# One kernel, two written-out orders of the same 4,431 steps

## The chip, the cores and the metric

The kernel runs on one core of one Trainium2 chip. The metric is device time in microseconds (us) of one execution; a kernel's time is the median of several runs. The engines are PE (TensorE, matmuls), DVE (VectorE), ACT (ScalarE), POOL (GpSimd) and SP (SyncE, which here only starts DMAs). Each engine works through its own list in the order in which the program was written.

## The reference

Inputs are queries, keys and values of 8 batches x 8 heads x 512 positions x 64 (`q_l`, `k_l`, `v_l`), 32 global positions per head (`q_g`, `k_g`, `v_g`), and two weight matrices.

```python
s_g = scale * q_g @ concat(k_g, k_l).T          # global queries see all keys
out_g = softmax(s_g) @ concat(v_g, v_l)
s_ll = where(abs(i - j) <= 32, scale * q_l @ k_l.T, -1e9)
out_l = softmax(concat(scale * q_l @ k_g.T, s_ll)) @ concat(v_g, v_l)
x = concat(out_g, out_l)                        # to 4352 x 512: heads side by side
out = gelu_erf(x @ w_in) @ w_out                # 512 -> 2048 -> 512
```

All of it is fp32.

## The kernel before

**The work.** Attention is cut into 64 units (batch, half of the 512 positions, pair of heads), the MLP into 17 chunks of 256 rows: one for each (batch, half) and the last, "g", for the global rows. Nearly every fp32 product is done as three products of fp32r halves: a copy rounds a value (high part), a subtraction leaves the rest (low part). So each product brings a copy (ACT or DVE) and a subtraction (POOL or DVE) with it.

**Steps.** `graph()` names 4,431 steps. The ones that the text below speaks of:

- Of a unit: `lk`, `lq`, `lv` load keys, queries, values; `lh` loads the global queries of a batch (lines 741, 865); `tk`, `tq` transpose (on PE for the first eight units, L819 to L827); `k1`, `q1` copy and `k2`, `q2` subtract (L605 on ACT, L607 on DVE, L612 the subtraction); `s` is the score product (L906), `m` masks it and finds the maximum from PSUM (L925), `b` scales that (L931), `e` is exp on ACT (L779), `n` sums up and normalizes (L955, L956, L959), `nf`, `ns` fill edge tiles (L966, L971), `t` transposes (L980 to L983), `ah`, `al` split the result out of PSUM (L605, L1000), `vm`, `vc`, `vl` ready the values, `o` is the product with the values (L1017, L1030), `c`, `x` put it together (L1043, L1048, L1049).
- Of the weights: `wl` loads one of 32 pieces of 512 KB (L630, L634), `w1` to `w3` pack it (L639 to L651), `w4` copies the high part, `w5` subtracts (L612, tile `wl`).
- Of the MLP: `h` (in parts `hc`) and `mo` are the two products of the first five chunks (L1206 to L1212, L1352 to L1362), `g` is gelu on ACT (L779), `gh` copies its high part (L605 or L607), `gl` subtracts (L612). From the sixth chunk on two chunks at a time share sums and differences of the weights, made once: `sw`, `ss`, `sh`, `sl` compute these, `sx`, `ya` write them to DRAM (tile `wd`), `rl` fetches 512 KB of them (L1275, `rt<-wd`, 168 times), `ft`, `fh`, `fl` make the matching sums of x, and `P` is the product (L1314).

**Order.** `SEQ` is a packed list. `plan()` unpacks one number for each step: number divided by 6 is the step's place in `graph()`, the remainder is the engine. The main loop emits the steps in this order and ties each instruction to the one emitted before it on its engine, so an engine's list is the list of `SEQ` filtered by engine. `DUR`, `LAT` and the due times in `graph()` play no part when the kernel runs; the data dependences, the counts of buffers and the lists do.

**The port wait.** `PORT` names the kinds of step which on DVE read or write SBUF alone. After such a DVE step the next POOL step in `SEQ` gets a semaphore wait on it:

```python
if x["on"] == "p" and not x["size"]:
    if shared:
        tc.add_manual_dep(ins[seen], shared, ... reason="port")
    shared = None
elif x["on"] == "v" and x["port"]:
    shared = ins[-1].name
```

There is no wait in the other direction: a DVE step that comes after a POOL step in the list is not held by a semaphore until that is done.

**Buffers.** PSUM has six tiles that turn among scores, transposes and hidden sums (`u`), five SBUF tiles turn among `g`, `gh`, `gl` (`gg`). `FORMS` names, of 33 numbered weight slots, the ten whose tile is taken from the pool `wq` and not from `wp`; these slots are used again for other data later.

Of the kernel before, what the change touches and what calls it, by code (L numbers as in the profile page):

```python
# [138 lines left out]
JOINT = {"s": "u", "t": "u", "h": "u", "gh": "gg", "gl": "gg", "gf": "gg"}
FORMS = (3, 5, 7, 9, 17, 19, 21, 23, 25, 27)  # L140
# [8 lines left out]
    "KF>Z(fc-l`l@hY(gt;Xd?axEb*|{5v?&bGO-z*bX=ca3Cfjr@`aEe*nkf8h8>Z^Uyte;3kj8a|QVm{5(8>NFcI^ZseopKHz#_6k+pts=!r1&qeq(co`9>8mRgU*^9h^R8-xD&qBIA`+?`H{GLgOYQz^+_uy|"
    "<eO<K(c^eq<M5`VlS0d&h7a)5PFvN63A0qDgchxcEuT@Ck8pJ!uSCMZaUqoy`EJvz<0F(l~5jnex45E0csQ&_yUc6U}UR&h=ja9)=H>&0%GM*HWjXDT4qlY{tPY{hk2~bIN9#}?4(K+--$SJ5Fk<SB{AO;X_"  # L150
    "kRG@dNkmOV(=lbxd%#*R9*9NIKx))s#5B}q&vwra<WkTsBo$}{@-cq_r=a&DIhZY=(;z8o2*Cz@i~xW~JRbsQpiQV2&=-gb(2kmoK7gFyQDP+EX4Ep!NyL1#6*G#EV0IuD1K&hH1g=5%fcAJ!Bfkf32Z6yG("
    "0!<_z*9gV=ojQd^f+RQ2M#_9I*;(7Lf{Z;zh@TskSC711kz)Udv0T{Ae<N?@;>GfhUXQ4JeW;r81_2ibI?<uP81P)22DX0P(W-5^9lMD^e^Z?5pRHEm^N?(v<mzHu^nBFL?L&Br-Ob)C%|mvbWaaT4qgKuK>"
    "vXr!}fVb&_}RqQL90FKw2;ja2WkH7=yhI!hz}7c^((wTkzND<5)9z3LuBsjv2%Ok!eg0+>Kf2c^CXFcnrP7^Bh>|6?<0zmU&iqPN2ES5x{ECdQZ%I88Gg-jb>r>-bLV<m}fAPF>_GourHuCfv;o5$Rpr7Kmg"
    "F`9mk&YAgTmdZPgsiYp8Xo1sEB21xkZ0cn#R;fXmoM>?H3K^kvWIm^Faw9tdVJW(lgt>&7OkK0w{}JXbZ}dmp_N^KR85?|sikTo^mk`xa&ZbEHazT#B9Qy;JoiW*>$HbOI*>b;$QH7Gw){5VHqx8|y?q_Kac"
    "t$W6Fcfy0<#)Kc$U@9zM7)qwX128sC;cM`MG`y=Wz;5L+{Dvo^}o3A2ZGT0tp7j^{o3+5bZ6bJU+#lBSal&=q8!EV7}aAz<T+=o>st9IcYR$08$uq2$@`v&$gb_~~tU4RGUUd6BVZt$+b{>L{NyUDu>e+J0J"
    "&BH@#ws;TW=3@Ck1a2X=1t`SL^}#?pyo1<jz<>J|<Co*FVU`0oVx^!LeP01T!g{@RxD&WI=rnE+|FUnF7gaL}r@-lOeV{9-h!<A_@m<EDd={JycM(YNxp4v9=h(M>3EY_)4CraxI^XX&X3Yhhs74E-`l7h)*"
    "bjVJ&`jKV(0<UU_ZH|i-v<01>~0jf=1rds{~RcX8^(`$xiuevp5XSO?%=lK6*X6CcHxhB@6-T@eK->MZ`@(fJRHk+!VAIwhWZnQ!t;F+pB+plyofu5x(_1Ync#2mANjoCF7QG8E8wqu3<4Ry&&R{>#J`SH`C"
    "Rz<gcB$xeko2<bJ}~sE5T0!Z}Tbf5yJQQlX!E@6|bYlhd1Ca)`am<{0;A6-%8vUz8f`*NN4aJggf3O{z1(aFogI&@B^>E=9mxLLT>p1d=U@u8GLzsTg^2*hmfrC)G%7Cz6xI0@}uuA>IK3LywfKnocG<qzd}"
    "&9Oe77~_<RrX|Dd3ROFnH27>ywQ=F1R(gg<>SG#1Sz_L4%r&%oRk41qut6RE`Mqyph*Fd3~PvWV~1{D+jS86zwu@xfg+5<<*pYneuvN3yg`tmz|cCF+UGNIir}_|>G|8h6VSLfYqViL|H)@s@&*g%$yfgaX+"
    "@oQnUT#zt@v%%FR|Ov?~yX3YxHdXk?|YUwBR)qF<O`vEOZBG3OhVP4H<l8^WX;XA^MHLD4)*I4}%TJ{jc{!eO_)=X*XBZi49YqpXG3EOL?w~UY`lGT2fze1i%{DCl1^FHD0n!`1HEqh2Z%2>?|@_e$_4{GTp"  # L160
    "pQu?tj1rT?gQU%bNyI%Zv&oCdsFtZj17!zce~X54sO1#lc*}lL$nT`2{FjMf>RG}P@>x=z_%iVlDMZQpFB7g2I{X7<E5%DWMw-{Ml3XG3$=68>TPFFJ631Hxi0jF35!aGq6b$t?={+Ki`T_YC;S2I0ah&uw="
    "~MDm;*ypvWC8VD%WmR*!ZZG1;v>?smL9*DJW2$TPZCMwQSyKNQ2>HEMm|D4K)l?dAQP!f@);tWyrN}wOOkSwc#DW57bv|HK+Q}Fn|g=HCS7mQlfNhb$6uj5B+95J@;LPbb$!cF%jTBtEwB17QElYgEh8-(X{"
    "&*AC=2`t{3rcq{kN$=(oz5YmIvf2%5m~J>NvTX{ENShoFqT+|Kb0Qsvw;w|4x3{A0!J%_o>4)Kwt~)u3tsHLw?79%|DrPg}mGkAw5rdiSoDw><3ePR6NB*wNc&FA{7#N+mE220{s+f)qaYaR7=@Kd(YoM`pE"
    "wsg-Yq9E~oG*Vd^T%1S-N$2&|=iNco<!ffA?U{6A90XlT+D>SvTk)UA~Dbg~~zI~zdIh_v05=~N==H01*2D&;SVh+!qoqRyeNrtYA<OC6=%q%i%|04wkw{Wa<e>I>8(G#pLCSVDb7*+^xQrh*j=en3tW(p;o"
    "%)M2WhbU83WJx-fU)6s4PLZsgV0H&E{V|?P51itj2rgf0MqF$$gf^z~Rem{djyFla895hv6LBLHjG5)0aX>P_9S~dM%;7Q;anjx^C8ewEe@Zba5R62q=gSI%3r9GjMnTtUC{iI+U4Z@5uX43lu|D|!6V}QvF"
    "6x|w_#z@lU(Fk-LGs7s;@Ie}VA?+0!lfFFQ47^Db)0xaU^b$kF<kDvY254((eGD0M0z(*_PhS;q(sfKd-51zeWu>>!=Q33Em+1eaudba}Yi6#mbu*d47Z^ZbnWP9VtnH@<>5FSCRlHy*kfM(=t^)@HAJJFQ9"
    "n4p2m)CBgFJUZWY^>cF_?D4iW|;wIEbtj!A8ZH~=w)U)Pzb!qum@+bKB<k;ch^<|QRdI|F{U@Tit!!eea3G3aP1&t8{@Oui}V+Rn;9dF9~gUU=dmUSrUqsOh67`@*XgrauLlFcZu&&#h1#uwC9G476|6t#S8"
    "LY<KM1}TJOOgDv%#aaI|FAJ&oEyNPG>G;MS!PjZ`MwxpQ&BR^s)Pxml&_H+JdhzcL%OB-U`0M{3Q4s^RL>~tVPTqdwcLOGZh?U4KRmTqx6yBW>%8j72Fe~bJjB_1#dC-2Zxx4g4<bT_62a1eLVQEHpjltxC;"
    "IQyf<)+b%HsO&F35p>|~7xj|Tn%AE1BC{ElU2UFO(XK-S;jFPKN^AGW^L3S$AP$LVg?JvxSUD)4lWz=Bl=SSrpqYX@_biLd^o^<0p{!Bo?#*(@vP0iDVkY<<7=a`5xkSwR7-iXml5I3d>c;5pV;EDeiO-O1X"
    "|l2pf7s%jYH5z|opZ1BrgYqg;Ib`Z<%VKr5^R8L`}80OX*Mu`=vUJ!i3OjR2=j@DmU-?z?Sds?rtoSZ4F+3cH~n=Crx9*e>*R_|?{T78`}t9n;myxPMVX9ip6RzGH)XI^2>XD?)jI8&;BXD+B-!#=|XvF``z"  # L170
    "?8m`}oEYb&>hD^?t<hF!?K{<J4y+EreumRueV4PbdS~@3>^Ip}bthYe?A_IOm|RA(7127t-dFugE3S1#wSv95dVBT3>a(riSLZlat4HfLu&=fvYW1~*PIv7lHm2^cRt|fA-KpxE)wxzJ`&b<a@(KGF_JnFP`"
    "&`|jx^9lQw%j_I^J5(x!tW%vUaouCx}D8zz13>y{F;q{5Fx*^xvg&A>S|C()JlUWS|_$TJ8iuC)#s{3kP$Y%Rt*_r|H0-!sI}HwT`M$Xf)MJ$wai*c9lfr%bw=y#*4u19qz!VI&8wBvexByk(L$H2)pZ_-pz"
    "iCmk9UGSlfw=vAotmENEWg$U4-o95<4*=LFXI}qw_zICu~w^0cR^G#*5Y-PHSq({KwTujxh8&X98q?D}f{LOx1qDjdjk06lx2+*CB607IPZwOq~wMqSkWl($+PQLg%|_SKYc$h_@6n&^oC$#gm309Dm(6+@+"
    "kUo$k)5wG|$RZw#60hC=HhfzJ7Ly3qTOc<0BEk3){o04Gv+t!`iFP^i>-yY9uhA3|S2-s8N*0dl4MIi2_G{?)m-6VC00B<l7<206o=>7BbcIPOo7QO<86CjUHS2IK%|7X-*V0y)WfT(^jOlryh0UH1yNQ1>f"
    "j2gDijg?j21LC$a{@|M&MrTc1+rAgeg>E9t+>lxhF>jt<}>TW?+a6jNqtGgZgI}{3yr{T~O5EK97^cwEH^yPG4T`aV!GaXu9_csIp{Vk1$3iyT47OsZBfjgCl4bS5JnV!$v+PR<0<*uuHy>nIFr|Fk?b9h5_"
    "HvaN@5jV+Ia{uJ^^B_<bbZ;jW`cYk;yQK3l_epwt-CMlXoe#JtxbJpqxF)Wh3+i<8H+BAxM-FfA^l<(BU7g6zRrN<Z*Vdou3~<x@L0*Kvzq2-cyz^$~&iW6+zjneh@7BlpMShf9;#TuE)zdTQI-llF;EwaQg"
    "*Nh@<=*bBgm%@B)z9DxG9U3K@K4ll;f-_u?%ctf#s_2&ne*H)d7p>obI<V)@HCmx`m;PVZ!eFKIm%;Z4%h#}vt*v)pRRXjCWrd?Ux&`si!z79y3CKEE8Hc5EA=<(f8%*FINtsGdHg%|%LO-hcX*fhctLCCN&"
    "QFshrCP%%72l6lRG8Tmsuv58oJJpWd;Sg3{vn%W?^Pn0OX$wRWiSZW`!uc-VBQe5n%X>`G1B9^(!*3W;SPLXSh77V3pt|KPh~JzbNxhh*ZCt-_O6tKOYwJK;d=#Px*H<kNFz~TLnY>JsD8_%FH{NIU$x{V`e"
    "9RL8v6$$4As3;;VRDGQ0W5_z^*EJzuahQyqCqIL<$m=@5tnqnVtrPpA+~5b6a@0&&EXMTR-`R>2oxO5{kUE-VZ$4($+37pg=io==b#%o7#`22nD*K=?2ttT&64;oXA%&|X1Va71uW@Nsxz7L@%(utc~_I8m@"
    "Xv?}Bgtq@)nJQ4-!74@HmR|%scUv@M+Bb%<jDbR-R3LGMP_!)sed{S^C{9i#NyiOPp)eAooE)bj%{38Ge4}^z=vjj;|JPZ+L!Vs}F><j-KmJ7EDfnu7l6h1B<5r(s9;e>Fso+HfGUkN`5ch?ide}q}$JHkD}"  # L180
    "jEE@wTev8zsoyUwi%?>fuqt8@HVRvW6!ExtN;o2%C`xCiiyG?P!d_7^i;D2YXT*<%)uLBK&x#HTUlh$3IqI*8f6N>ePR{-)91z8%cf~737sb=VBC)UjlSobErnoPBNw`)tq5hHhoN!+F>H1k&m3T(|b)iEH6"
    "Afh3(wx*F#)xVo>qU#R8?q!3Q&cCKC>;}7#UG2jVv%S_v@m=`@`WfQ-XYqO1xVV(bF($sl=yp5UwwUKR0NYO31cKH#JjRo$#eC`Ma#l7q{_&75nE!66vS6VWhqf2lZ}g3gqLT37u^wU%&rdiO4SmnL?D4?-x"
    "fcNyq!IpnJuk|vDtUT>%*5aJ0nkt4YIA-Ua?a)L%gW|tB6K6PkJP4iFhL+*~!ShEIS*Gm?XbtgxUASRvEj^CyPYfk(lgCc8mOoe1$X_u}Rz#Y4$<(zv7p~yR(a=3&d-ro5cO%En-G?OnxSEDdLlSCN^f5O10"
    "ULWI(z>TGe(myIZ_k(jm!3rbsf9qzsbVBri%PNPf(IEIpU~x1=EZK)PLCk=e7ovK`XNvTNCI#O286@>!CXWHV*Y%l61`XY1QukigrH%XdlVNFHV9$ks^?iV3-!(sOcHZerxRoRJ%se<S@%x<tay5p#oz{Zc{"
# [1283 lines left out]
```

## Time and profile before

| | before |
|---|---|
| median of 3 runs | 1049.62 us (1047.58 to 1050.57) |
| profiled execution | 1046.37 us, span 1044.6 us |
| PE busy | 1000.1 us, 96% of the span |
| PE weight loads busy | 870.8 us, 83% |
| DVE busy | 800.9 us, 77% |
| ACT busy | 706.8 us, 68% |
| POOL busy | 488.3 us, 47% |
| DMA | 175.06 MB, mean 168 GB/s |

The span runs from the first to the last instruction of the profiled execution; that execution's own time is 1.8 us longer. An engine's busy time is the union of its instructions' times. Matmuls are pipelined and their ends are modelled, so PE can be "busy" while it runs below its pace. The times of DVE instructions are measured from start to end, with whatever holds one inside.

### The profile page before, as it was taken

What the parts mean: (1) busy time and instruction counts of PE and PEld (TensorE: products, weight loads), DVE (VectorE), ACT (ScalarE), POOL (GpSimd) and SP (SyncE); (2) the same over time, 40 slices, a digit from 0 to 9 for tenths busy, and PEclk for the clock granted to TensorE, in tenths of its full rate; (3) what the DMA queues carried; (4) which work ended last, traced back from release to release, by engine and by line L of the source; (5) the groups of instructions that cost most, each with busy time, mean ns of one, the idle gap of its engine ahead of it and who ended that gap; (6) DMA issues with size and microseconds to landing.
All of it is one profiled execution on the core that took longest, in us unless ns stands there. A gap on an engine that the chain in (4) does not pass through costs nothing.

```text
span 1044.6 us, 21336 instructions
## 1 busy us (share of the span) xinstructions
PE 1000.1 (96%) x6712; PEld 870.8 (83%) x6712; DVE 800.9 (77%) x2206; ACT 706.8 (68%) x1660; POOL 488.3 (47%) x506
## 2 busy tenths in 40 slices
...
GB/s 225 251 294 142 37 65 47 105 83 115 139 113 119 189 238 231 283 213 108 168 203 250 159 155 157 209 218 115 157 235 207 142 162 191 231 188 171 197 146 41
DMA packets 307729, 175.06 MB, mean 168 GB/s; under 512 B 256256, under 2 KB 279040, under 8 KB 307616
## 3 DMA queue, kind: packets, MB, share of 16 engines
...
## 4 chain that ended last, share of the span: by engine, by line
PE 46%; DVE 15%; DMA 5%; issue 4%; ACT 3%; SPq 2%; POOL 0%; DVEq 0%; POOLq 0%; ACTq 0%
PE hb L1314 17%; PE acc L1360 6%; PE acc L1361 6%; PE acc L1362 6%; PE o L1017 2%; PE s L906 2%; DMA raws<-in_v_l_dram 1%; DMA rt<-wd 1%; DVE at L1000 1%; PE t L980 1%; DVE a_t L925 1%; DVE k L612 1%; DMA raws<-in_q_l_dram 1%; DMA vr<-in_v_l_dram 1%; PE h L1210 1%
## 5 line engine op out<-in xcount | busy, mean ns | idle before, releaser
L1360 PE MATMUL acc<-wh,gh 128*128 128x512 f32 x512 | 205.8, 402 | 0.0
L1361 PE MATMUL acc<-wh,gl 128*128 128x512 f32 x512 | 201.6, 394 | 1.0 <-POOL gl L612 1.0
L1362 PE MATMUL acc<-wl,gh 128*128 128x512 f32 x512 | 200.8, 392 | 0.0
L1314 PE MATMUL hb<-fh,rt 128*128 128x256 f32 x960 | 182.9, 282 | 2.6 <-DVE hb L1332 1.2
L612 POOL TENSOR_TENSOR gl<-gf,gh 128x512 fp32r<-128x512 f32 x80 | 105.7, 1321 | 168.6 <-PE acc L1362 46.3
L1314 PEld LDWEIGHTS hb<-fh,rt 128*128 128x128 f32 x960 | 152.2, 189 | 5.7 <-DVE hb L1332 1.8
L1314 PE MATMUL hb<-fl,rt 128*128 128x256 f32 x480 | 134.3, 280 | 0.0
L779 ACT ACTIVATE a_t<-a_t,sm 128x192 f32<-128x192 f32 (+1 forms) x256 | 117.1, 459 | 11.6 <-DVE sm L931 10.4
L1362 PEld LDWEIGHTS acc<-wl,gh 128*128 128x128 f32 x512 | 96.6, 189 | 21.2
L779 ACT ACT_TABLE_LOAD x81 | 103.9, 1283 | 11.6 <-issue 3.8
L612 POOL TENSOR_TENSOR vs<-vr,vs 128x512 fp32r<-128x512 f32 x56 | 75.5, 1348 | 77.4 <-DVE vs L607 15.7
L1360 PEld LDWEIGHTS acc<-wh,gh 128*128 128x128 f32 x512 | 97.1, 190 | 16.1 <-ACT ob L605 0.4
L1361 PEld LDWEIGHTS acc<-wh,gl 128*128 128x128 f32 x512 | 96.8, 189 | 16.2 <-POOL gl L612 1.9
L1314 PEld LDWEIGHTS hb<-fl,rt 128*128 128x128 f32 x480 | 90.3, 188 | 1.4 <-POOL fl L612 0.2
L925 DVE CUSTOM_DVE_ANT_0 a_t<-s,mask 128x192 f32<-128x192 f32 (+1 forms) x256 | 82.1, 364 | 11.0 <-PE s L906 10.7
L612 POOL TENSOR_TENSOR gl<-gq,gh 128x512 fp32r<-128x512 f32 x47 | 63.0, 1340 | 54.4 <-PE acc L1362 15.1
L1314 PE MATMUL hb<-xf,rt 128*128 128x256 f32 x576 | 77.9, 289 | 3.2 <-ACT gf L779 2.3
L605 ACT ACTIVATE at<-t 128x512 fp32r<-128x512 f32 (+1 forms) x112 | 59.3, 541 | 31.6 <-PE t L983 16.8
L1017 PE MATMUL o<-at,vs 128*128 128x256 f32 x448 | 70.1, 286 | 10.2 <-DVE at L1000 4.0
L1314 PEld LDWEIGHTS hb<-xf,rt 128*128 128x128 f32 x576 | 74.2, 196 | 6.7 <-ACT gf L779 2.5
L612 POOL TENSOR_TENSOR vgs<-raws,vgs 128x640 fp32r<-128x640 f32 x32 | 55.0, 1718 | 47.9 <-issue 11.6
L1210 PE MATMUL h<-xh,wh 128*128 128x256 f32 x256 | 73.8, 288 | 1.4 <-DVE xs L1049 0.7
(197 smaller groups left out, 2433.8 us busy)
## 6 DMA issues: line engine op xcount, KB each, us to landing
rt<-wd SPq DMA_DIRECT2D x168, 512.0 KB, 4.4
...
raws<-in_k_l_dram SPq DMA_DIRECT2D x224, 36.0 KB, 2.4
raws<-in_q_l_dram SPq DMA_DIRECT2D x224, 32.0 KB, 2.1
...
```

The costliest lines, as they stand in the source:

```text
L605: nc.scalar.activation(out=out, in_=in_, func=AF.Copy)
L612: (nc.vector if e == "v" else nc.gpsimd).tensor_sub(**kw)
L779: nc.scalar.activation(func=func, **kw)
L906: nc.tensor.matmul(out=st[u, "s", jj][:, c:c + w], lhsT=qq[pr, qt * P:qt * P + P], rhs=kk[pr, k0:k0 + w], start=(i == 0 and n == 0), stop= ...
L925: nc.vector.tensor_tensor_reduce(out=a_t[:, j, aoff[half][i]:aoff[half][i] + w], in0=s[:, c:c + w], in1=masks[half][i], scale=1.0, scalar= ...
L980: nc.tensor.transpose(out=t[:, n * P:n * P + P], in_=a_t[:, j, c:c + P], identity=ident)
L1017: nc.tensor.matmul(out=o[:, :, qsl], lhsT=l.rearrange("p s e -> p (s e)"), rhs=r, start=(n == 0), stop=(n == 3), skip_group_check=True)
L1210: nc.tensor.matmul(out=h, lhsT=hi, rhs=xh, start=(c == 0 and f % 2 == 0), stop=False, skip_group_check=True)
L1314: nc.tensor.matmul(out=h[:, r], lhsT=a, rhs=b, start=(i in (1, 5) and r == 0 and c == 0 and n == 0), stop=(c == 1 and n == 2), skip_group_ ...
L1360: nc.tensor.matmul(out=acc[t], lhsT=gh[:, f % 2, tsl], rhs=hi, start=(f == 0), stop=False)
L1361: nc.tensor.matmul(out=acc[t], lhsT=gl[:, f % 2, tsl], rhs=hi, start=False, stop=False)
L1362: nc.tensor.matmul(out=acc[t], lhsT=gh[:, f % 2, tsl], rhs=lo, start=False, stop=(f == NF - 1))
```

## The change

`SEQ` and `FORMS` are replaced, nothing else. The diff, cut to its core:

```diff
-FORMS = (3, 5, 7, 9, 17, 19, 21, 23, 25, 27)
+FORMS = (3, 5, 7, 9, 11, 15, 19, 23, 27, 32)
...
 SEQ = (
-    "c-jrpiDMFk;s9U<jQbup3>Yx(`yMc0z<>b*#u(SQ$CyvemipAUd}?N9X0~k4%uH>X*|KG(X12_1sZCQ;Q(NYhnwpuKsj2Dj_x%l@6>5k2q2tgzECB@r+)zIB3RDDbgC2)Ygk_)#KpA=-nt?$96QN&1<<MT}E"
...
+    "c-jrriDME3<1k<bj2i}w`yMc0+&7H-8ZcnM7~>lE81tQGrl!8jpDi;pGh4RI%+#itnXj6fnVOj`H8nLgwPjv;rDkfTrl#Nb{1J}@YKInJqtF1<1LZ@%h9;pRXgl-@^f>f9Gz+ajWzat81ZWm^1FD6-3cU*j1"
...
 )
```

Unpacked as `plan()` unpacks them, both strings hold the same 4,431 steps:

| list | steps before | steps after | in the same order in both (longest common part) |
|---|---|---|---|
| PE | 1031 | 1031 | 563 |
| ACT | 1122 | 1177 | 351 |
| DVE | 1365 | 1336 | 450 |
| POOL | 401 | 375 | 222 |
| SP | 512 | 512 | 290 |

Steps that change engine, as "from, to, how many": `gh` DVE to ACT 43, ACT to DVE 19; `k1` DVE to ACT 20, back 10; `vc` 20, back 10; `q1` 16, back 9; `w4` 16, back 6; `w1` ACT to DVE 14, back 4; `w5` POOL to DVE 7, back 2; `sw` POOL to DVE 6; `ss` 6; `sl` 3, back 1; `ft` 10, back 1; `fl` 10, back 10; `xl` 3, back 2; `ns` DVE to POOL 15, back 12; a few others one or two each.

Other counts of the two lists, before and after. Changes between exp and gelu on ACT's list, each of which needs a table load: 82 and 70 (the first load among them). POOL steps that do arithmetic (no loads, no memsets): 361 and 335; of these, the next DVE step in the list is one of the `PORT` kind after 183 and 145. POOL steps that get the port wait: 236 and 213.

By stretch, each ending with a chunk's last `mo` step (POOL arithmetic steps; of these, how many are followed by a `PORT` step of DVE; DVE steps):

| stretch that ends with the last `mo` of chunk | before | after |
|---|---|---|
| (0, 1) | 34; 14; 94 | 32; 14; 83 |
| (1, 0) | 22; 6; 102 | 22; 13; 104 |
| (2, 0) | 31; 17; 83 | 20; 8; 78 |
| (2, 1) | 33; 16; 117 | 29; 14; 121 |

First steps of SP's list before: `lk` of unit (0,0,0), `wl` 0, `lh` 0, `wl` 2, `lk` (0,0,2), `wl` 4, `wl` 1, `lk` (0,1,0). After: `lk` (0,0,0), `lh` 0, `lk` (0,0,2), `wl` 0, `lq` (0,1,0), `wl` 2, `wl` 4, `wl` 1, `lk` (0,1,0). On DVE the list began with `q1` of unit (0,0,1) and then `tg`, which needs `lh`; now it begins with `tg`, and that `q1` is on ACT. On POOL the load `lv` of unit (0,1,0) now comes behind `nf` and `ns` of unit (0,0,3), which were DVE's.

## Rows read from the trace of the kernel before

**Rows 1.** Page: shares of the chain of waits that ended last, by engine.
```profile
PE 46%; DVE 15%; DMA 5%; issue 4%; ACT 3%; SPq 2%; POOL 0%; DVEq 0%; POOLq 0%; ACTq 0%
```
**Rows 2.** Windows: PE, PEld, DVE, ACT, POOL busy (instructions), PEclk, DMA share, GB/s.
```profile
0.00:26.00 26.00, 18.86 (x80) 12.77 (x80) 11.28 (x49) 14.10 (x41) 16.27 (x39) 1.00 1.00 225
...
104.00:182.00 78.00, 72.20 (x469) 57.66 (x468) 76.03 (x180) 56.93 (x130) 54.48 (x52) 1.00 0.25 50
182.00:312.00 130.00, 127.64 (x931) 114.55 (x928) 111.22 (x346) 97.43 (x237) 53.47 (x59) 1.00 0.46 111
312.00:416.00 104.00, 96.58 (x651) 85.03 (x649) 100.69 (x226) 72.53 (x170) 73.94 (x71) 0.98 0.70 195
416.00:884.00 468.00, 452.09 (x3189) 402.70 (x3189) 399.59 (x1134) 341.08 (x815) 218.80 (x212) 0.99 0.69 184
884.00:1014.00 130.00, 130.00 (x858) 119.19 (x857) 32.73 (x67) 51.25 (x101) 36.21 (x29) 1.00 0.61 197
```
**Rows 3.** Groups by form, DVE, whole span: xcount | busy us, mean ns.
```profile
L959 DVE TENSOR_TENSOR a_t<-a_t,sm 128x512 f32<-128x512 f32 x64 | 59.6, 931 | 2.2
L925 DVE CUSTOM_DVE_ANT_0 a_t<-s,mask 128x224 f32<-128x224 f32 x128 | 49.0, 383 | 0.0
...
L612 DVE TENSOR_TENSOR k<-kt,k 128x320 fp32r<-128x320 f32 x56 | 38.0, 679 | 4.0 <-ACT k L605 3.2
...
L607 DVE CAST wh<-wf 128x512 fp32r<-128x512 f32 x17 | 11.8, 714 | 0.0
...
L612 DVE TENSOR_TENSOR wl<-wf,wh 128x512 fp32r<-128x512 f32 x8 | 6.5, 807 | 0.1
```
**Rows 4.** Groups by form, DVE, from 0 to 104 us.
```profile
L925 DVE CUSTOM_DVE_ANT_0 a_t<-s,mask 128x224 f32<-128x224 f32 x20 | 7.7, 385 | 0.0
...
L959 DVE TENSOR_TENSOR a_t<-a_t,sm 128x512 f32<-128x512 f32 x9 | 6.2, 692 | 0.3
...
L607 DVE CAST wh<-wf 128x512 fp32r<-128x512 f32 x4 | 1.7, 420 | 0.0
...
L612 DVE TENSOR_TENSOR k<-kt,k 128x320 fp32r<-128x320 f32 x3 | 1.5, 488 | 0.1
```
**Rows 5.** Groups by form, DVE, from 104 to 182 us.
```profile
L959 DVE TENSOR_TENSOR a_t<-a_t,sm 128x512 f32<-128x512 f32 x5 | 6.6, 1327 | 0.2
```
**Rows 6.** Groups by form, POOL, whole span.
```profile
L612 POOL TENSOR_TENSOR wl<-wf,wh 128x512 fp32r<-128x512 f32 x24 | 32.1, 1337 | 15.6 <-DVE wf L651 7.6 <-DVE k L612 2.2 <-DVE sm L931 1.6
```
**Rows 7.** Timeline of SP, start: start us, us, what.
```profile
4.62 0.60 SPq L630 DMA_DIRECT2D wraw<-in_moe_w_in_dram  x1
5.26 1.93 SPq L741 DMA_DIRECT2D qg<-in_q_g_dram  x4
```
**Rows 8.** Timeline of DVE, start: also [idle before, releaser].
```profile
11.93 0.31 DVE L865 STREAM_TRANSPOSE qg<-qg 128x128 f32<-128x128 f32 x1 [5.40 <-DMA qg<-in_q_g_dram]
```
**Rows 9.** Timeline of PE, start.
```profile
7.93 3.14 PE L906 MATMUL s<-kt,qt 64*128 64x192 f32 x16
13.12 0.69 PE L827 MATMUL qp<-ident,rawb 128*128 128x128 f32 x2 [2.06 <-DVE sm L925]
```
**Rows 10.** Timeline of POOL, 20 to 75 us.
```profile
36.51 1.07 POOL L762 DMA_DIRECT2D vr<-in_v_g_dram  x2
```
**Rows 11.** Timeline of PE, 50 to 55 us.
```profile
52.36 1.96 PE L1030 MATMUL o<-ao,vr 128*64 128x128 f32 x16
```
**Rows 12.** Groups by form, ACT, whole span.
```profile
L779 ACT ACT_TABLE_LOAD x81 | 103.9, 1283 | 11.6 <-issue 3.8 <-PE hb L1314 1.8 <-PE h L1212 1.5
L605 ACT ACTIVATE gh<-gf 128x512 fp32r<-128x512 f32 x43 | 27.0, 627 | 12.9 <-PE acc L1362 11.2 <-PE acc L1361 0.9 <-POOL gl L612 0.3
```
**Rows 13.** Waits: who waited for whom, total us, times, longest.
```profile
POOL gl L612 <- DVE gh L607: 39.3, 12, 9.8
```
**Rows 14.** Waits of PE.
```profile
PE acc L1361 <- POOL gl L612: 1.0, 2, 0.6
```
**Rows 15.** Windows: the stretch with the busiest DMA engines.
```profile
52.00:78.00 26.00, 25.00 (x128) 16.86 (x128) 21.26 (x72) 22.84 (x55) 7.28 (x13) 1.00 0.94 293
```

More of the change, by code (lines that the diff above doesn't have):

```diff
@@ L149 @@
[L149 to L184, printed above, removed]
@@ new lines @@
+    "0F*AV3VN_VF1`0P%vx=dKXrK&4e$8$^lUL3s5p_IdmoTIoLE<3NRB212AEqLDxWM0+6uj@aeF*@Ku1bu<xK-p?ugZm>4z}rh?VL(SRd>ebBprAs8Mu2%{miFca)B^j)|bKmefNAH)6!^TS-Q%`jHYD}Y(>?X"
+    "X)dA_M_$0EA#Pco(1qcni*l6A%fctL7Wn`!E}T1CPT-VEbX0U@-3~*ciZ3m;wF?zzUbZ@3p)RSOWLJgYcE`2Y?0yw}#_A23QXec(1}X!`tC&;2Yq7!iHf#z%kx9JOeMmg*8${FFcCe3(q4L0MziY$fs~EVhd"
+    "n9{AYl-hTuI89|!j!Qpl^waW!JJ)H?}I^X`V55Q8<rnqS~S#CiBd__mreH9g3`kugLq;tt$_xCTE5n1H;A%po4YVL+o-3bc72x6DDh&<WtbfXB$i2#+_30M}FyJ8Sw7&msDOD}mFH0k7H%L(D)fLtLl<dRHM"
+    "PBi=+lTl0Jk&NmC$k9Y}z^u3B$h?JxG=zYMU8YNI(6RVkC13*Q+6x91j7zzda5czG*9iR@VL6bnMkq*!ruL=Dz@Jh`=;0z!JML@k*a}e<|a6K~Norl=q{Tz7@7(%Z>WPr<SQt16P6_6iYhj<&oMtz1T06n1j"
@@ new lines @@
+    "pbDCXk)XCBwjy^Tw|Kuo2v9Nf4sRZ<LVbtC0sGKo-$u}3#4+T}8VYbc>Lg-3I_tFnIhfO+{{gE&0GNP0fE+<gLGv*`0>$9j=()h@=rH&Z@Ga20AS&o*<Yu4|rNq2}-tA?B_Ib-*JE{dW4SWjN3$kFgfbL+#7"
+    "!Y^}4FruM&LhTnPa~fJk&%9s4$}&{iV%P<BBP-3-t8b4rW17zG!xD9F?|m(F|ZsQMlAuqho0=6gxUpOhMo-aVs0S%y^k?r46JS`=nPr|hJy)pFMzvHhrDr2KPrP+h29NXi$3n%g#Ha(MAafMf%2H=FiCI^rW"
+    "Z98!$!UYrU7n%fOP}jE$C4%3du!|!=USyf&W6xz>I*g;D?AKbtdpf;Mv~gC?IlwT^_9PT|v(Qe-Ca#&hswtF7oa`|A}4;rqy`>OT8<-=e*ydn|w#W9lr5^EtrCjRo4LM@&y4(<YBZHdA#mjzzOtz^d0osy35"
+    "`hb%MGXsIk87fT_L}D4p*Tpx5`J?*V!;Kw3A^XGYHSjn=(|y5W6_egy@uSq9jSnT46-b0O!UhOu)oy8)N$?$piq{Q=O_%*T9+8p0%NkeHWhhJ0(WA7dbx#XfZ%w&rWhM>X$b@R<2^z5YcgQ%yf^HFh1QweE0"
```

94 lines of the change are left out of this document (61 added, 33 removed).

## The prediction, made before the changed kernel ran

> **What bounds the kernel now.** I read the chain of waits first. PE makes up 46% of it, DVE 15%, DMA 5%, ACT 3%, POOL nothing [rows 1]. So PE sets the pace, DVE is what it is late for, and ACT and POOL count only through these two.
>
> Next I cut the span into stretches [rows 2]. From 884 to 1014 us PE is busy without a gap while DVE is at a quarter of its time: nothing is to be won there by any order. Before that PE has gaps: 7.1 us up to 26 us, 5.8 of the 78 us to 182, 2.4 of the 130 to 312, 7.4 of the 104 to 416, 15.9 of the 468 to 884. The two stretches with the worst shares (7.4% and 7.1%, against 3.1% in the 598 us of the two ordinary ones) are those in which DVE is busy for 97% of the time (76.0 of 78, 100.7 of 104) and in which POOL is busy for 70%, against 40 to 50% elsewhere.
>
> Gaps are only part of PE's loss, since matmul ends are modelled. A second gauge is the weight loads (PEld): in the gapless stretch they are busy for 119.19/130 = 0.917 of the time. At that pace the four stretches would need 62.9, 124.9, 92.7 and 439.1 us, so they lose 15.1, 5.1, 11.3 and 28.9 us, 60 in all against 31.5 of gaps. The mix of matmuls differs between stretches, so I use this as the outer bound and the gaps as the inner one. The Trainium skill (Perfetto Trace Analysis, Identifying the Most-Contended Engine) says that busy matmuls are no measure of the room left, and that the busy share of the weight loads is; by that rule the larger figures hold, and the sum below would be twice as large.
>
> Why is DVE full? The same instruction takes very different times [rows 3, 4]. L959 takes 692 ns early, when POOL has little arithmetic, and 931 on average; the k subtraction 488 and 679; the wh copy 420 and 714. In the first crowded stretch L959 takes 1327 [rows 5]. L925, which reads PSUM, takes 385 and 383: it is not stretched. So DVE's steps on SBUF alone stand still while a POOL step runs, up to its 1.3 us [rows 6], and the trace counts that as busy DVE. In these three groups alone it comes to 64 x 0.239 + 56 x 0.191 + 17 x 0.294 = 31 us.
>
> **The change, part by part.** No arithmetic is added or removed, only engines and orders change.
>
> *DVE and POOL.* POOL loses 26 steps, 26 x 1.337 = 35 us of held port. DVE loses 61 copies net (`gh` 24, `k1` 10, `vc` 10, `w4` 10, `q1` 7) of 420 ns at most [rows 4], some 23 us, and gets POOL's 23 subtractions net, the six double `ss` and ten `w1`, at 0.5 to 0.8 us each (0.807 for `wl`, waiting included [rows 3]), some 20 us. I take DVE's own work as unchanged. What changes is how often it runs into POOL: the next DVE step behind a POOL step is one on SBUF alone 145 times instead of 183.
>
> Stretch 312 to 416 holds the chunks (2,0) and the start of (2,1). For (2,0) the POOL steps fall from 31 to 20 and such neighbours from 17 to 8, DVE's steps from 83 to 78. If its gaps fall to the ordinary 3.1%, they go from 7.4 to 3.2 us: -4.2; by the weight loads, from 11.3 to the ordinary 5.7%, 5.9: -5.4. I take -4.5; at worst 0, if PE's gaps there come from elsewhere.
>
> Stretch 104 to 182 is mostly chunk (0,1): POOL 34 to 32, neighbours 14 and 14, DVE's steps 94 to 83. Here DVE has less to do, but as many collisions, and chunk (1,0) behind it gets 13 instead of 6. To the ordinary share it would be 5.8 to 2.4, -3.4; by the weight loads 15.1 to 4.4, -10.7; at worst +3, seven more collisions of 0.4 us, about the mean stretch of a port step that the sums above show. I take -2.5, near the inner bound.
>
> Everywhere else neighbours fall from 183-14-17 = 152 to 145-14-8 = 123, by 19%. If PE's loss in the ordinary stretches follows, it is 18.3 x 0.19 = 3.5 by gaps, 34.0 x 0.19 = 6.5 by weight loads, and 0 if these gaps have other causes. I take -4.5.
>
> A rule speaks against this part. The Trainium skill (Perfetto Trace Analysis, Optimizing Scalar/DVE Operations) warns that moving work between DVE and GpSimd might not help, since they share a port. The row says that a step holds the port for 1.337 us on POOL and 0.807 on DVE [rows 3, 6], so that moving 26 of them frees 26 x 0.53 = 14 us. By the rule the first two terms vanish; this is a rival below.
>
> *First loads.* Now `wl` 0 is issued ahead of the four loads of `lh` (4.62 and 5.26 us) [rows 7]; these land at 11.9, and DVE, whose list has `tg` in front of the first `m`, waits 5.4 us for them [rows 8]. The scores that `m` needs start at 7.9, and PE waits 2.1 us behind `m` [rows 9]. In the new list `lh` goes ahead of `wl` 0: 0.64 us earlier, and without 512 KB in front of it in a stretch where the DMA engines are busy all the time (share 1.00) [rows 2]. The first score product is half of the 3.14 us, so `m` could start at 9.5 and not at 12.3. Gain between 0.6 and 2.8 on DVE, and on PE no more; it is 0 if the scores' successors wait for `wl` 0 instead. I take -1.5. On POOL's queue `lv` of unit (0,1,0) is put behind two edge steps. Its last issue ends at 37.6 [rows 10], and the product that reads it starts at 52.4 [rows 11]: 14.8 us of cover for 1.3 us of steps and the landing. Cost 0; without the cover, 1.3. All other loads wait for buffers on SP's list as before: 0, with the DMA rival's 5 as the far end.
>
> *ACT.* It gets 55 steps net, some 30 us at 0.4 to 0.63 each (`gh` 627 ns), and loses 12 table loads of 1283 ns, 15.4 us [rows 12]. That is +15 us, 2% of its busy time, on an engine with a third of the span idle and 3% of the chain: +1, from 0 to the 15. `FORMS` picks the pool of ten slots: 0, no instruction depends on it.
>
> **Sum.** -4.5 -2.5 -4.5 -1.5 +1 = -12 us. The profiled execution took 1046.4 us, so 1034.4; the median of the runs, 1049.6, is 3.2 above it, so 1037.6 in terms of medians. I forecast 1037.
>
> **The rivals.**
>
> *Twice the gain.* PE's hidden loss goes as well: -5.4 -10.7 -6.5 -2.8, with ACT at 0, is -25.4: 1024. For it speaks that DVE's stall is many times PE's gaps; against it that half of the collisions stay.
>
> *The exchange between DVE and POOL is worth nothing* (the rule above). The first two terms go: -4.5 -1.5 +1 = -5: 1045. Against it: stretches with much POOL are those with much loss.
>
> *The stall is hidden anyway.* POOL's `gl` waits 39 us for copies on DVE [rows 13], yet PE waited only 1.0 us for `gl` [rows 14]; there is stock between the engines. Then less stall only means more idle DVE, and the time stays: 1047 to 1052. Against it: DVE's 15% of the chain. That the list does not do on the chip what its neighbours suggest, because nothing holds a DVE step behind POOL but the port itself, ends here too.
>
> *DMA.* The busiest stretch moves 293 GB/s at share 0.94 [rows 15]; a fetch of 512 KB more takes 1.8 us there. If the new list bunches three more of the `rl` fetches where the writes of `wd` run, that is 5 us: 1042, inside the forecast's own range.
>
> *ACT becomes late (slower).* Place: `gh` in front of `gl` and `mo`. 43 copies go to ACT, 0.627 instead of 0.420 us, and queue there behind exp groups and table loads: about 0.2 + half a load, 0.64, is 0.85 us later each, 36 us in all. It decides once more than a third reaches PE: then it eats the 12. With half of it, 18: 1037.6 - 1 + 18 = 1055. For it: ACT's list grows by 5%. Against: the 1.0 us that PE now waits for `gl`, and the saved table loads.
>
> **How the numbers follow.** Forecast with its own range of 1030 to 1043 (the DMA rival in it): 0.50. Twice the gain: 0.12. Exchange worth nothing: 0.10. Hidden: 0.15. ACT late: 0.13. A measurement of this kernel can tell 0.3% from no change, about 3 us: faster means below 1046.5, slower above 1052.8. So faster 0.50 + 0.12 + 0.10 = 0.72, same 0.15, slower 0.13. The range of 1023 to 1052 leaves out about half of the doubled gain and nearly all of the late ACT, 0.06 + 0.12.
>
> **What would show it.** Right: L959's mean falls from 931 towards 800, wh and k likewise, L925 stays at 383; POOL's busy time falls by some 35 us, table loads to 69 on L779; PE's gaps between 312 and 416 fall to about 3 us; the first `m` starts before 11 us. Wrong: means of DVE's SBUF steps as now (the order does not avoid POOL); means down but PE's gaps as now (hidden); waits of `mo` or `gl` for ACT's `gh` that grow by 10 us or more.

## The result, and the profile after

The new list takes 1015.32 us (median of 4 runs, 1013.26 to 1017.72); the old one, run beside it on the same chip, 1048.65 (1047.58 to 1050.57). The ratio is 0.968, with an interval of 0.965 to 0.971: 33 us faster. The prediction had the sign and the mechanism and less than half of the size: 12.6 us, a range that ended at 1023. The profiled executions took 1046.37 and 1016.96 us, 29.4 apart; the differences below are between these two.

The page after, busy times of the engines and shares of the chain of waits:

```profile
PE 987.0 (97%) x6712; PEld 865.3 (85%) x6712; DVE 745.0 (73%) x2184; ACT 715.9 (71%) x1703; POOL 444.9 (44%) x473
...
PE 71%; DMA 14%; DVE 8%; SPq 3%; ACT 2%; issue 2%; POOL 0%; DVEq 0%; ACTq 0%; POOLq 0%
```

DVE lost 56 us of busy time and POOL 43. PE lost 13 us of busy time, though it does the same matmuls, and its idle time in the span fell from 1044.6 - 1000.1 = 44.5 to 1015.2 - 987.0 = 28.2, by 16. So the 29 us were as good as half visible as gaps and half hidden in matmuls that ran below their pace. The two chains cannot be laid side by side as they stand. The shares of before [rows 1] add up to 75% only, because that chain is followed back no further than 254.5 us from the start; those of after add up to 100%. Of the part that is covered, 75%, PE had 61%, DVE 20% and DMA 7%; after, PE has 71%, DVE 8% and DMA 14%. So DVE fell and PE rose, and the loads are what is late next.

The stretches of [rows 2] after; columns as there:

```profile
0.00:26.00 26.00, 19.20 (x101) 13.36 (x102) 14.30 (x58) 15.13 (x45) 16.84 (x41) 1.00 0.90 217
104.00:182.00 78.00, 75.87 (x519) 64.27 (x518) 72.70 (x186) 62.28 (x152) 51.56 (x51) 1.00 0.26 53
182.00:312.00 130.00, 129.84 (x945) 117.20 (x944) 112.10 (x349) 102.71 (x253) 54.07 (x59) 1.00 0.49 116
312.00:416.00 104.00, 101.30 (x725) 90.92 (x724) 94.84 (x238) 79.74 (x177) 50.63 (x48) 1.00 0.82 234
416.00:884.00 468.00, 457.75 (x3260) 411.62 (x3259) 364.16 (x1113) 349.59 (x840) 206.35 (x202) 1.00 0.72 189
```

PE's gaps went from 5.8 to 2.1 us (104 to 182), 2.4 to 0.2, 7.4 to 2.7 (312 to 416) and 15.9 to 10.2; in each stretch it also began more matmuls than before. The granted clock is the same, a mean of 0.995 before and 0.997 after, of the upper of its two levels (2.4 GHz): the clock is no part of this.

Groups by form of DVE after, to be read against [rows 3]; xcount, busy us, mean ns:

```profile
L925 DVE CUSTOM_DVE_ANT_0 a_t<-s,mask 128x224 f32<-128x224 f32 x128 | 49.2, 384 | 0.0
L959 DVE TENSOR_TENSOR a_t<-a_t,sm 128x512 f32<-128x512 f32 x64 | 46.7, 730 | 2.2
...
L612 DVE TENSOR_TENSOR k<-kt,k 128x320 fp32r<-128x320 f32 x56 | 38.5, 687 | 3.7 <-ACT k L605 2.8
...
L931 DVE TENSOR_SCALAR sm<-sm 128x4 f32<-128x4 f32 x64 | 21.2, 331 | 0.6
...
L607 DVE CAST wh<-wf 128x512 fp32r<-128x512 f32 x7 | 4.1, 592 | 0.0
```

L959 fell from 931 to 730 ns, close to its quick 692; L925, which reads PSUM, stayed. The other steps on SBUF did not all follow: the wh copy fell from 714 to 592, the k subtraction did not move (679, 687), and L931, a scaling of 128x4 numbers, got worse. Its row of before:

```profile
L931 DVE TENSOR_SCALAR sm<-sm 128x4 f32<-128x4 f32 x64 | 17.6, 275 | 0.6
```

A sum over all of DVE: take for each form the time that a quarter of its instructions stay under, and call what others take above it stall. It was 140 us before, with 156 instructions over 200 ns late; after, 81 us and 91 instructions. 140 - 81 = 59 us is about the 56 us by which DVE's busy time fell, so DVE's own work hardly changed. Nearly all of the 59 us come from two places: the copies of L607 (205 instructions with 36.7 us of stall before, 140 with 11.2 after) and the steps `n` and `nf` (L955, L959, L966: 38.9 us before, 8.9 after). The subtractions of L612 stand behind POOL as they did (35.7 and 33.2 us).

One stalled instruction of before shows what a stall is. DVE's timeline (start, us), and POOL's around it:

```profile
159.96 1.67 DVE L959 TENSOR_TENSOR a_t<-a_t,sm 128x512 f32<-128x512 f32 x1
```

```profile
156.78 4.30 POOL L612 TENSOR_TENSOR wl<-wf,wh 128x512 fp32r<-128x512 f32 x3
```

Three subtractions on POOL follow each other from 156.78 to 161.08. L959 starts in the third and ends at 161.63, 0.55 us after POOL: most of its work, 0.69 us when free, was done once POOL had ended. Over the trace of before, all 19 instances of L959 that began during a subtraction of POOL were late, 45 of 58 casts of L607, 41 of 59 subtractions of L612; of 119 L925 and 51 L1000, which read PSUM, none. Of the 156 late instructions all but two ran beside a step of POOL. But not every DVE step on SBUF alone is held, as the text ahead of the result has it: of 93 transposes (L788, L789, L832) that began during a subtraction of POOL, none was late, and of 12 reciprocals (L956) none. The transposes are not among the kinds that `PORT` names, the reciprocal is a part of `n`.

What PE waited for, sums over the view of waits: DVE 22.2 us before and 7.0 after, POOL 6.7 and 1.2, ACT 4.4 and 5.1, DMA 5.3 and 9.5. Its longest lines after (who waited for what: us, times, longest):

```profile
PE hb L1314 <- DMA rt<-wd: 4.7, 5, 2.1
PE qp L827 <- DMA raws<-in_q_l_dram: 4.4, 2, 4.3
...
PE acc L1361 <- POOL gl L612: 1.0, 1, 1.0
```

The `gl` wait is as in [rows 14]: ACT's extra copies do not show in it. The `rt` waits are new at this size (0.9 us before): they are the fetches that the DMA rival named.

Where the gain is collected, by chunk: the last `mo` step of a chunk began earlier than before by 3.0 us for (0,0), 6.7 for (0,1), 7.4 for (1,0), 12.7 for (1,1), 18.8 for (2,0), 21.4 for (2,1), 22.5 for (4,0), 29.5 for (6,0) and 29.3 for the last. A chunk's end does not stand behind quite the same work in both lists. At (3,1) the lead is only 12.4 us, since 3,839 matmuls have begun before it after and 3,779 before; where these numbers agree, at (4,1), (6,1) and the last chunk, it is 20.5, 29.9 and 29.3. So the lead grows all along the kernel, until POOL and DVE have little left to do.

### The profile page after: what moved, and what is told of

It is laid out like the page before. It is cut to its first block, busy times and chain, and to the rows that moved or that the text cites. A ratio compares the mean times of both kernels' runs of the same rounds, so it can differ in the third digit from the quotient of the medians.

```text
span 1015.2 us, 21336 instructions
## 1 busy us (share of the span) xinstructions
PE 987.0 (97%) x6712; PEld 865.3 (85%) x6712; DVE 745.0 (73%) x2184; ACT 715.9 (71%) x1703; POOL 444.9 (44%) x473
## 4 chain that ended last, share of the span: by engine, by line
PE 71%; DMA 14%; DVE 8%; SPq 3%; ACT 2%; issue 2%; POOL 0%; DVEq 0%; ACTq 0%; POOLq 0%
PE hb L1314 18%; PE acc L1360 9%; PE acc L1361 9%; PE acc L1362 9%; DMA rt<-wd 4%; PE o L1017 4%; PE s L906 4%; PE h L1206 2%; PE h L1210 2%; PE t L980 2%; PE h L1211 2%; PE h L1212 2%; PE acc L1352 2%; DMA raws<-in_v_l_dram 2%; DMA raws<-in_q_l_dram 2%
## 5 line engine op out<-in xcount | busy, mean ns | idle before, releaser
L1361 PE MATMUL acc<-wh,gl 128*128 128x512 f32 x512 | 200.8, 392 | 1.1 <-POOL gl L612 1.0
L612 POOL TENSOR_TENSOR gl<-gf,gh 128x512 fp32r<-128x512 f32 x80 | 105.3, 1316 | 204.8 <-ACT gh L605 48.6
L779 ACT ACTIVATE a_t<-a_t,sm 128x192 f32<-128x192 f32 (+1 forms) x256 | 117.1, 460 | 11.2 <-DVE sm L931 10.4
L1361 PEld LDWEIGHTS acc<-wh,gl 128*128 128x128 f32 x512 | 96.6, 189 | 16.1 <-POOL gl L612 1.7
L612 POOL TENSOR_TENSOR vs<-vr,vs 128x512 fp32r<-128x512 f32 x56 | 73.8, 1319 | 83.2 <-DVE k L612 13.0
L925 DVE CUSTOM_DVE_ANT_0 a_t<-s,mask 128x192 f32<-128x192 f32 (+1 forms) x256 | 81.8, 366 | 11.0 <-PE s L906 10.2
L612 POOL TENSOR_TENSOR gl<-gq,gh 128x512 fp32r<-128x512 f32 x47 | 63.4, 1349 | 52.9 <-PE acc L1362 22.0
L1000 DVE TENSOR_TENSOR at<-t,at 128x512 fp32r<-128x512 f32 (+1 forms) x112 | 67.3, 615 | 14.0 <-ACT at L605 13.2
L1314 PE MATMUL hb<-xf,rt 128*128 128x256 f32 x576 | 74.8, 281 | 0.0
L1314 PEld LDWEIGHTS hb<-xf,rt 128*128 128x128 f32 x576 | 71.1, 189 | 1.4
```

The costliest lines, as they stand in the source:

```text
L612: (nc.vector if e == "v" else nc.gpsimd).tensor_sub(**kw)
L779: nc.scalar.activation(func=func, **kw)
L925: nc.vector.tensor_tensor_reduce(out=a_t[:, j, aoff[half][i]:aoff[half][i] + w], in0=s[:, c:c + w], in1=masks[half][i], scale=1.0, scalar= ...
L1000: nc.vector.tensor_sub(out=at[:, 1], in0=st.pop((u, "t", j))[:, :n * P].rearrange("p (n q) -> p n q", q=P), in1=at.bitcast(F32)[:, 0])
L1314: nc.tensor.matmul(out=h[:, r], lhsT=a, rhs=b, start=(i in (1, 5) and r == 0 and c == 0 and n == 0), stop=(c == 1 and n == 2), skip_group_ ...
L1361: nc.tensor.matmul(out=acc[t], lhsT=gl[:, f % 2, tsl], rhs=hi, start=False, stop=False)
```

## The experiments

Theory A in the expectations: the gain is DVE's SBUF steps standing behind POOL's arithmetic less often. The rivals stand with each run. Ratios are to the kernel before, run beside each.

**Order and engines taken apart.** A step has a place in the list and an engine. One kernel keeps the old places and takes the new engines, the other the reverse (the edit in words):

```diff
-SEQ = (old order, old engines)
+SEQ = (old order, each step on its engine of the new list)     # e1, FORMS as before
+SEQ = (new order, each step on its engine of the old list)     # e2, FORMS as after
```

> The old list of steps in its old order, each step on the engine that the new list gives it (POOL 335 arithmetic steps instead of 361, ACT 55 steps more). Theory A (the gain comes from where the steps stand, so that DVE's steps on SBUF meet POOL's less often): little of the gain, 1038 to 1050 us, DVE's L959 still over 850 ns. Rival B (the gain comes from the change of engines: POOL's 26 steps fewer): most of it, below 1028 us, whatever the order.

> The new order, each step on the engine that it had in the old list. Theory A: at least half of the gain stays, 1014 to 1032 us, L959 below 800 ns. Rival B: the gain goes, over 1038 us.

Measured: e1 1068.35 us, ratio 1.019 (1.016 to 1.022); e2 1056.13, 1.008 (1.005 to 1.012). Both are slower than the old list. Theory A missed both times, since the new order alone brings nothing. Rival B, by which the engines carry the gain, had e2 right (over 1038 us) and e1 wrong (below 1028). Neither half carries a part of the gain. Yet the stall fell in both, to 108 and 105 us (122 and 132 late instructions). Each half removes its own part of it: the new engines that of the copies (18.2 us in e1, 28.0 in e2, 36.7 before), the new order that of `n` and `nf` (27.6 in e1, 11.8 in e2, 38.9 before). L959 of e1 and of e2 (groups by form; their lines are numbered two lower):

```profile
L957 DVE TENSOR_TENSOR a_t<-a_t,sm 128x512 f32<-128x512 f32 x64 | 55.4, 866 | 2.2
```

```profile
L957 DVE TENSOR_TENSOR a_t<-a_t,sm 128x512 f32<-128x512 f32 x64 | 48.5, 758 | 2.2
```

But PE waited more: for DVE 32.8 and 23.8 us, for POOL 10.7 and 10.2, against 22.2 and 6.7 with the old list. PE's longest waits in e1:

```profile
PE t L981 <- POOL ge L969: 6.1, 5, 2.1
PE qp L825 <- DMA raws<-in_q_l_dram: 4.5, 2, 4.2
PE o L1015 <- DVE at L998: 3.3, 3, 1.2
```

So the amount of stall does not set the time. An engine that works through a fixed list holds everything behind a step that must wait, and a list whose engines belong to another order has more such steps at its head. That last sentence is argued; the rise of PE's waits is shown.

**The port relieved.** POOL's subtractions read one eighth of their columns; a memset on POOL writes zeros to the rest, so most of the low parts that POOL makes are left out. Order, engines and waits stay. e3 has the old list, e4 the new one. (The slices are written shorter here than in the kernel.)

```diff
 def sub(e, **kw):
+    if e == "p":
+        o = kw["out"]
+        nc.gpsimd.memset(o.bitcast(F32)[..., o.shape[-1] // 8:], 0.0)
+        kw = {k: v[..., :v.shape[-1] // 8] for k, v in kw.items()}
     (nc.vector if e == "v" else nc.gpsimd).tensor_sub(**kw)
```

> The old list, but POOL's subtractions read an eighth of the columns and fill the rest with zeros (that part of the products is left out), so that POOL reads SBUF for a fraction of the time. Theory A (PE was late because DVE stood still behind POOL): at least 20 us faster than the old kernel, 1010 to 1028 us, L959 near 700 ns. Rival C (DVE's stall was covered; the new list wins by PE's own order, by fewer table loads or by earlier first loads): within 10 us of the old kernel, 1038 to 1050 us, though L959 falls.

> The new list with POOL's subtractions cut in the same way (an eighth of the columns, the rest zeros). Theory A: the two lists come close to each other, e4 within 10 us of e3, and e4 less than 15 us below the new kernel: 1000 to 1014 us. Rival C: e4 stays some 25 us below e3.

Measured: e3 1008.37 us, 0.963 (0.960 to 0.966); e4 1011.04, 0.966 (0.962 to 0.970). The old list loses 40 us, all that the new one had gained and 7 more. The new list loses some 4, which is not clear of the noise: the interval of e4 overlaps that of the kernel after (0.965 to 0.971). So run, the two lists are alike. The chain of e3, and its groups of DVE:

```profile
PE 84%; DMA 7%; DVE 3%; SPq 3%; ACT 1%; issue 1%; POOL 0%; DVEq 0%; POOLq 0%; ACTq 0%
```

```profile
L961 DVE TENSOR_TENSOR a_t<-a_t,sm 128x512 f32<-128x512 f32 x64 | 45.1, 705 | 2.2
...
L614 DVE TENSOR_TENSOR k<-kt,k 128x320 fp32r<-128x320 f32 x56 | 27.8, 497 | 6.1 <-ACT k L603 5.2
```

L959 (here L961) is at 705 and the k subtraction at 497, its quick time [rows 4]; the stall is 24 us (19 in e4), and PE waits 7.1 us for DVE, as with the new list. The old order was not bad in itself: POOL's work made it late. That zeros are quicker to multiply is no rival: the product with `gl` (L1361, here L1363) takes 392 ns in e3, 394 before and 392 in the kernel after, which has no such zeros.

**Port, or only POOL's shorter steps?** In e3 a POOL step is also shorter. e5 and e6 give its length back without reading: twelve memsets of one column behind each subtraction.

```diff
     (nc.vector if e == "v" else nc.gpsimd).tensor_sub(**kw)
+    if e == "p":
+        for _ in range(12):                     # e5, e6; 3 in e10, e11
+            nc.gpsimd.memset(<last column of o>, 0.0)
```

> The old list with POOL's subtractions as in e3 (an eighth of the columns, zeros in the rest), and twelve one-column memsets behind each, so that POOL takes about as long as in the old kernel (some 1.3 us a step) but reads SBUF for a quarter of that. In e3 two things went at once, the held port and POOL's own latency. If the port did it: still below 1020 us, DVE's L959 (two lines lower or higher here) near 700 ns. If POOL's latency did it: 1035 us or more.

> The new list with the same subtractions and the same memsets. If the port did it: within 8 us of e5 and below the new kernel's 1015 by no more than 10. If POOL's latency did it: about as the new kernel, and 20 us or more below e5.

Measured: 1198.21 us (1.143, 1.139 to 1.146) and 1125.97 (1.072, 1.069 to 1.076). The dose was wrong. The pad of `gl` in e5, POOL by form, and what it did to PE:

```profile
L617 POOL MEMSET gl<- 128x1 f32 x1524 | 158.1, 104 | 80.5
```

```profile
PE acc L1366 <- POOL gl L617: 31.7, 32, 4.5
PE o L1022 <- POOL vs L617: 28.6, 19, 4.4
```

One memset takes 104 ns and a pause of 80.5/1524 = 53 ns, so twelve add 1.88 us, and a POOL step takes some 2.7 us in place of 1.3. By the letter of the expectations e5 lies on the side of POOL's latency, and e6 on neither; but with steps twice as long as before, the two say nothing on the port. They do say that a doubled POOL step makes POOL itself late: PE waits 123 us for it in e5.

With three memsets the length is nearly that of before:

> As e5 with three one-column memsets behind each subtraction and not twelve. In e5 a memset took 0.157 us with its pause, so that a POOL step came to 2.7 us, twice the old kernel's; now it should be 0.35 + 0.48 + 0.47 = 1.3 us, as in the old kernel, with the port held for reads only 0.35. If the port did it: below 1025 us. If POOL's latency did it: 1035 us or more, with L959 near 700 ns all the same.

> The new list with the same padding. If the port did it: within 10 us of e10, and 1005 to 1016 us. If POOL's latency did it: near the new kernel's 1015 and 20 us or more below e10.

```profile
L612 POOL MEMSET gl<- 128x448 f32 x127 | 61.3, 483 | 224.8 <-PE acc L1367 76.1 <-DVE gh L605 48.2 <-PE acc L1366 22.3
L617 POOL MEMSET gl<- 128x1 f32 x381 | 39.9, 105 | 14.6
L614 POOL TENSOR_TENSOR gl<-gf,gh 128x64 fp32r<-128x64 f32 x80 | 28.6, 357 | 10.1 <-ACT gh L603 10.1
```

Those are e10's rows on POOL: 483 + 357 + 3 x (105 + 38) = 1269 ns for one `gl`, near the 1321 ns of the same step before. (Other steps came out 4 to 14% short: `wl` 1290 for 1337 ns, `vs` 1252 for 1348, `vgs` 1483 for 1718.) Measured: e10 1008.03 us, 0.964 (0.960 to 0.967); e11 1008.43, 0.963 (0.959 to 0.967). POOL's steps are nearly as long as before, and the 40 us stay away. What is left of the difference in length does not matter either: from e3 to e10 a `gl` went from 0.84 to 1.27 us, and the time stayed (1008.4 and 1008.0). It is POOL's reading of SBUF, the port.

The Trainium skill (SBUF — State Buffer, Who interferes with whom) says that a DVE step with two SBUF inputs contends with a GpSimd step that reads SBUF and not with one that only writes it, while casts can, in a mode that takes both pairs of ports, contend with POOL too, and that whoever starts first holds the other up. The trace of e3 agrees on what contends: of 22 two-input subtractions that began during a memset of POOL none was late, of 23 casts 9 were, by 2.6 us together. That POOL is held up in turn is not shown here.

**Where along the kernel.** e7 takes the new list up to the last `mo` of chunk (0,0), 576 steps, and then the old list; e8 the old list up to there and then the new; e9 the new up to the last `mo` of (1,1), 1,477 steps, and then the old (the edit in words).

```diff
-SEQ = X
+SEQ = X up to the last mo of a chunk, then all other steps in the order and on the engines of Y
```

> The new list up to the last mo of the first chunk (576 of 4,431 steps, 122 us), then the old list for all that is left. Theory A (the gain is collected all along the kernel): 2 to 5 us faster than the old kernel, since the new one is 3.0 us ahead at that place. Rival E (the first loads set up the rest): 20 us or more.

> The old list up to the last mo of the first chunk, then the new list. Theory A: 1015 to 1022 us, what the new kernel takes and the 3 us of its start. Rival E: over 1035 us.

> The new list up to the last mo of chunk (1,1) (1,477 of 4,431 steps), then the old one. There the new kernel is 12.7 us ahead. Theory A (each stretch gains by itself): 1033 to 1041 us. Rival (the two lists do not join, or the gain is made good later): 1045 us or more.

Measured: e7 1045.79 us, 0.998 (0.9954 to 0.9997), about 3 us and between 0.3 and 5; e8 1015.70, 0.968 (0.965 to 0.971), all of the gain, to within some 3 us, without the new start; e9 1037.16, 0.991 (0.989 to 0.994), about 10 us, against a lead of 12.7 us at that point. All three lie where theory A had them. A lead once won is kept, nearly; the first loads are not needed for the rest.

**Less left for the port.** With the new list one of the groups that wait longer than before is L931, step `b`. e12 takes the step out: `m` finds the minimum of the negated and scaled scores, and exp takes that as its bias. The port wait that stood on `b` goes to the port step before it.

```diff
-    scale=1.0, scalar=-3.0e38, op0=ALU.add, op1=ALU.max,
+    scale=-SC, scalar=3.0e38, op0=ALU.add, op1=ALU.min,
...
-    nc.vector.tensor_scalar_mul(out=st[u, "mn"], in0=st[u, "mn"], scalar1=-SC)
+    pass
...
-    act(AF.Exp, out=v, in_=v, scale=SC, bias=...)
+    act(AF.Exp, out=v, in_=v, scale=-1.0, bias=...)
```

> The new list without step b: the mask step scales by the negative factor and takes the minimum, so that exp needs no scaled maximum. In the new kernel b (L931) takes 21.2 us, half of it behind POOL, 64 times between the mask and exp. Theory A (what still stands behind POOL still costs PE): 1003 to 1012 us. Rival: with the new list DVE has slack there, as e4 suggests, 1012 to 1017 us.

Measured: 1011.95 us (1010.68 to 1014.54), 0.967 (0.964 to 0.969) of the kernel before. The page of e12:

```profile
PE 984.3 (98%) x6712; PEld 863.9 (86%) x6712; DVE 734.6 (73%) x2120; ACT 715.8 (71%) x1703; POOL 445.4 (44%) x473
```

DVE has 64 instructions and 10 us less. The median is 3.4 us under that of the kernel after and well under that of before. The intervals of the two ratios overlap, so those 3 us are likely and not shown. And 1011.95 lies on the border between the two expectations (1003 to 1012, 1012 to 1017): the run does not tell whether what stands behind POOL still costs PE.

## Why the prediction was right in kind and wrong in size

**What bounds the kernel.** Right. PE sets the pace and DVE is what it was late for: its waits for DVE fell from 22.2 to 7.0 us. The chain's shares were read as shares of the whole span, and cover 75% of it; what was concluded from them holds for that part. That DVE's SBUF steps stand still behind POOL, and the trace counts that as busy, is shown by the late instructions above, and that it costs time by e3 and e10: with most of POOL's reading gone and the order unchanged, 40 us go. The prediction put it too widely: transposes and the reciprocal (L956), also on SBUF alone, are not held.

**DVE's own work unchanged.** Right: 59 us of stall against 56 us of busy time.

**Stretch 312 to 416, -4.5.** Its gaps fell from 7.4 to 2.7 us, to the "about 3" that was named. The lead grew by 6.1 us over chunk (2,0), some 1 us of it because the new list puts a few matmuls off.

**Stretch 104 to 182, -2.5.** Gaps 5.8 to 2.1; the lead grew by 6.7 - 3.0 = 3.7 us over chunk (0,1). Within its bounds. What the count of neighbours said there, "as many collisions", was wrong: the stall fell from 23.4 to 17.1 us.

**"Everywhere else neighbours fall from 152 to 123, by 19%", -4.5.** This is the step that failed. Outside of the two stretches stall fell from 87.6 to 47.2 us, by 46%, and the lead that arose there is 29.3 - 3.0 - 3.7 - 6.1 = 16.5 us, beside -4.5 + 1 in the sum. The step took the neighbours in the list for the collisions on the chip. Neighbours fell by 21% (183 to 145), instructions late by over 200 ns by 42% (156 to 91). The experiments show the count to be no measure even of the sign: counted in the same way e1 has 162 neighbours and e2 166, fewer than the old list, and both are slower. The list says which DVE step comes next behind a POOL step, not when: if DVE gets there after POOL is done, nothing is lost; if it gets there in the middle, up to 1.3 us are. That this is why the count was off by half is argued. The second error sat in the price of a collision: the value taken was near the inner gauge (gaps, 3.5) and not the outer (weight loads, 6.5). Had the outer gauge been multiplied by the stall's real fall, it would have given 34.0 x 0.46 = 15.6 us, beside the 16.5.

That product is no rule, though, and the runs say so. A fall of 32 us of stall (e1) went with 20 us lost, one of 116 us (e3) with 40 us won, one of 62 (e4 against after) with 4. These fit a stall that costs only where PE stands behind it. Nearer to the time was PE's own wait for DVE and POOL together: 43.5 us in e1, 34.0 in e2, 28.9 before, and between 7 and 13 in the kernels from 1008 to 1016 us (8.2 after, 7.7 in e3, 7.3 in e4, 12.5 in e12), which it does not rank among themselves. It is no price either: e9 has 27.4 us, hardly less than before, and is 10 us faster.

**First loads, -1.5.** The mechanism as told: `lh` is issued at 4.78 us, and DVE's first rows after are these (start, us; the last bracket is idle time and what ended it):

```profile
9.91 0.31 DVE L865 STREAM_TRANSPOSE qg<-qg 128x128 f32<-128x128 f32 x1 [9.91 <-DMA qg<-in_q_g_dram]
...
10.71 0.35 DVE L925 CUSTOM_DVE_ANT_0 a_t<-s,mask 128x192 f32<-128x192 f32 x1
```

The same `m` before:

```profile
12.40 0.35 DVE L925 CUSTOM_DVE_ANT_0 a_t<-s,mask 128x192 f32<-128x192 f32 x1
```

The first `m` starts at 10.7 in place of 12.4. At the end of chunk (0,0) the lead is 3.0 us, and e7 keeps about 3. But e8 comes to the same end without it, to within some 3 us: that it adds to the rest is not shown.

**ACT, +1.** ACT's busy time rose by 9 us, not 15, with 69 table loads as forecast, and PE's waits for it rose by 0.7 us (4.4 to 5.1). The term is below 1.

```profile
L779 ACT ACT_TABLE_LOAD x69 | 88.5, 1283 | 16.2 <-PE acc L1362 6.5 <-PE h L1212 3.6 <-issue 2.8
```

**The rivals.** "Twice the gain" (1024) was nearest, and for its reason: PE's hidden loss went too, 13 of the 29 us. It fell short by the same step, since it took the same 19%. The Trainium skill (Perfetto Trace Analysis, Identifying the Most-Contended Engine) says that the room left is read from the busy share of the weight loads and not from busy matmuls; the runs agree that gaps alone, 16 of 29 us, show too little. "The exchange between DVE and POOL is worth nothing" fell in a way that wasn't foreseen: the new engines alone are worse than nothing (e1), and with their own order they are part of a gain of 33 us. The Trainium skill's warning that such moves might not help (Perfetto Trace Analysis, Optimizing Scalar/DVE Operations) agrees with e1, which also moves copies from DVE to ACT, and not with the change as a whole. "The stall is hidden" is false for the old list, and nearly true for the new one: 4 and 7 us were left to win in e4 and e11, the first not clear of the noise, the second hardly. DMA: PE's waits for it rose by 4 us, near the 5 that were priced, and drowned in the rest. ACT late: it did not come.

**The signs that were named.** L959 below 800, L925 unchanged, POOL's busy time down (43 us, 35 named), 69 table loads, gaps of some 3 us and `m` before 11 us all came. The wh copy came part of the way (714 to 592); "k likewise" did not come.

**Open.** Which steps at the head of a list make e1 and e2 slower than the old list was not taken apart. Nor does any run show whether their loss comes from the port: neither was run with POOL's reading cut.
